# Attention tiles in pairs: one visit of the PE for two tiles, in a kernel of chunked attention and a low-rank mixer

## The chip, the cores and the metric

The kernel runs on one core of a Trainium2 chip. The metric is the device time of one launch, in microseconds (us). The profile shows TensorE as PE (matrix products) and PEld (loading of weights), VectorE as DVE, ScalarE as ACT, GpSimd as POOL, and SyncE as SP, which here only issues DMAs. A wait on a DMA queue's own issue is written SPq.

## The reference, cut to what matters

```python
B, H, S, D = 8, 8, 576, 64          # q, k, v; chunks of 64 rows
scores = scale * q_c @ k_c.T        # 64 x 64 for each chunk and head
attn = exp(scores - max) / (sum + 1e-9)
x = (attn @ v_c), heads side by side        # 8 x 576 x 512
h = x.transpose @ U @ V                     # rank 32, along the sequence
u = x + h.transpose
out = u + relu(u @ w_ch1) @ w_ch2           # 512 -> 2048 -> 512
```

All of it is float32 outside. The kernel splits the operands of the large products into a high and a low part and uses three products for one.

## The kernel before, in words

Two batches make a pair, and the kernel goes through four pairs (`pr` 0 to 3). The 1152 rows of a pair are nine tiles of 128 rows (`t` 0 to 8), and the tiles are three groups of three (`g` 0 to 2).

**The long work** is the last line of the reference, u through 2048 hidden columns. A group takes 16 blocks (`f`), and a block is 12 matmuls into one PSUM bank (`hidden`, tile `h`, L846), a relu on ACT that leaves the high part (`hh`, L854), a DVE instruction that leaves the low part (`hl`, L859), and 3 times 3 matmuls that add to three PSUM banks (`project_out`, tiles `o`, L872). The `o` of a block come after the `hidden` of the next one, so that the relu has time. Of each three `o` matmuls the third reads `hl`. After a group's last block DVE adds the three banks to x (L884) and SP sends x to the output (L887).

**The work beside it** belongs to the next pair. A tile's q and k are brought into blocks of 32 by DMAs on ACT's queue (`permute`), loaded by SP (`Tile.load`, tiles `qn` and `kn`, L695; tile 4 lies across two batches and takes four DMAs where the others take two) and transposed on DVE (`Tile.turn`, L703). Then PE makes the scores (32 matmuls of 64x64, L720), DVE subtracts the maximum (L733, L734), ACT takes the exponential (L740), DVE transposes it (`turn_ex`, L751) and sums it (`sums`, L745 to L747), SP writes it to DRAM in four DMAs (`put_ex`, L758) and reads it back in four (`get_ex`, L765, tile `eT`), and PE makes the values (32 more such matmuls, L773), which DVE scales into x (L785). `load_v` on POOL brings v (L710). The scores and values of a tile share two PSUM banks (`as`). When x is there, a projection per batch follows (`plan_proj`: `xh` on ACT, `xl` on DVE, two matmuls a tile into one bank, L586 and L587), then for each tile the mixer (`plan_mix`: one or two matmuls into a bank `u`, L633; an add on DVE, L639; a transpose on DVE, L808; four DMAs out, L816; one back, tile `uf`, L822; and a split into `uth` on ACT, L835, and `utl` on DVE, L836). `uth` and `utl` are the operands of `hidden`.

**What sets the order.** Every engine runs its instructions in the order in which the program lists them. Pair 0's attention and its first two groups are listed by a planner (`order`). There, two `hidden` in a row are often followed by two blocks of `o`. From group 2 of pair 0 on, plain loops list the work. In both, places are counted in steps: a block is four steps, one ahead of each of its three `o` groups and one behind them. Pair 0's groups 0 and 1 are steps 0 to 127 (`FIRST` = 128), group 2 is 128 to 191, and pair `pr` begins at `pr * PAIR` = 192 `pr`. The side work is put into a table by step (`at`), and the loops run what the table holds for a step.

**A visit** is what PE does for attention at one step. Before, `both` makes the values of one tile and the scores of the next in two banks; 28 visits serve the 27 tiles of pairs 1 to 3, the first with scores alone and the last with values alone. DVE's share of a visit is listed right there: two times maximum and subtraction, then two scalings.

**The pools.** PSUM has eight banks under one tag: three are held by the `o` sums, one or two by `h`, and `as`, `y` and `u` take the others for a while. `slot` buffers of 2 KB a partition (`NS` of them) hold all the small tiles, and `x` has `NX` buffers, freed when the output's DMA has read them.

Of the kernel before, what the change touches and what calls it, by code (L numbers as in the profile page):

```python
# [21 lines left out]
def kernel(  # L22
# [23 lines left out]
    NT = 2 * S // P  # L46
    GT = 3
    RUN = 8
    FAST = 3
    NX = 10  # L50
    NS = 8
    TB = 32
    k_in = k
    NQ = P // TB
# [5 lines left out]
    NPAIR = B // 2  # L60
# [10 lines left out]
    def bank(name):  # L71
        return psum.tile([P, 512], F32, tag="bank", name=name)
# [919 lines left out]
    def at(s, *runs):  # L992
        agenda.setdefault(s, []).extend(runs)

    def plan_tile(pr, t, s, before):
        a = Tile(pr, t)
        at(before + 2 if before >= s - 15 else s - 9, a.load)
        at(s - 4, a.turn)
        at(s + 1, a.load_v)
        at(s + 2, a.turn_ex, a.sums)  # L1000
        at(s + 3, a.put_ex)
        at(s + 6, a.get_ex)
        return a

    def plan_mix(pr, t, s, get=None):
        m = Mix(pr, t)
        at(s, m.low_rank, m.add)
        at(s + 1, m.turn)
        at(s + 2, m.put)
        at(s + 5 if get is None else get, m.get)  # L1010
        at(s + 10 if get is None else get + 8, m.split)

    def plan_proj(pr, e, i, s):
        if i == 0:
            projs[pr, e] = project_ops(pr, e, [None] * NT)[0]
        h, lo, product, *rest = projs[pr, e][i]
        at(s, h.run)
        at(s + 1, lo.run)
        at(s + (5 if i == 4 else 3), product.run, *(z.run for z in rest))

    projs = {}

    chain = [((1, t), FIRST + s) for t, s in enumerate((-51, -33, -11, 2, 15, 28, 42))]
    for pr in range(1, NPAIR):
        base = pr * PAIR
        chain += [((pr, 7), base + 4), ((pr, 8), base + 18)]
        if pr < NPAIR - 1:
            chain += [((pr + 1, t), base + s) for t, s in enumerate((34, 54, 74, 94, 114, 138, 157))]
    chain.append((None, (NPAIR - 1) * PAIR + 32))

    made = {}
    prev = None
    before = 0
    for key, s in chain:
        now = plan_tile(*key, s, before) if key else None

        def both(prev=prev, now=now):
            ps = [bank("as") for e in range(2)]
            if prev:
                prev.values(ps)  # L1040
            if now:
                now.scores(ps)
                now.softmax()
            if prev:
                prev.scaled()

        at(s, both)
        if prev:
            made[prev.pr, prev.t] = s
        prev, before = now, s  # L1050

    for pr in range(1, NPAIR):
        base = pr * PAIR
        if pr > 1:
            for z, e in enumerate(range(2)):
                for k in range(8):
                    at(base - PAIR - 26 + 42 * z + 5 * k, lambda pr=pr, e=e, k=k: permute(pr, e, [k]))
        s = made[pr, 4] + 1
        for i in range(5):
            plan_proj(pr, 0, i, s if i == 4 else s - 9 + 2 * i)  # L1060
        for t in range(3):
            plan_mix(pr, t, s + 8 + 2 * t)
        s = made[pr, 8] + 1
        for i in range(5):
            plan_proj(pr, 1, i, s if i == 4 else s - 9 + 2 * i)
        for t in range(3, 6):
            plan_mix(pr, t, s + 8 + 2 * (t - 3))
        for t in range(6, 9):
            plan_mix(pr, t, base + NF * 4 + 6 + 8 * (t - 6))

    for t in range(6, 9):
        plan_mix(0, t, FIRST - 45 + 2 * (t - 6), FIRST - 25 + t - 6)

    now = 0
    for o in plan:
# [55 lines left out]
```

## Time and profile before

| | |
|---|---|
| three timed runs | 935.1, 935.91, 936.25 us; median 935.91 |
| the profiled execution | 936.13 us, of which the span from the first to the last instruction is 934.4 |
| granted PE clock, mean | 0.996 |
| busy: DVE, ACT, POOL | 49%, 24%, 9% of the span |
| `h` matmuls, L846, 2304 | 338 ns each from start to end, started about every 175 ns |
| `o` matmuls, L872, 1728 | 396 ns each, started about every 233 ns |
| attention matmuls of pairs 1 to 3, L720 and L773 | 864 each; every matmul of the program appears as two |

Times are from the profiled execution; the matmuls overlap, so their starts say what one costs. In a row of the timeline stand the start, the length, the engine, the line and operation, the tile written and the tiles read, the shape and the count; brackets give idle time ahead of it and what ended that.

### The profile page before, as it was taken

How to read it: one execution, taken by the hardware profiler on the slowest of the kernel's cores; microseconds unless marked ns; L12 is line 12 of the kernel's file. 1: busy time of each engine (PE TensorE's matmuls, PEld its weight loads, DVE VectorE, ACT ScalarE, POOL GpSimd, SP SyncE). 2: the span in 40 equal slices, each digit the busy share in tenths (PEclk: the TensorE clock that was granted, in tenths of full speed). 3: DMA queues.
4: the chain of work that ended last, by engine and by line, in shares of the span. 5: the costliest groups of instructions: out<-in, count | busy, mean ns of one | idle time of the engine just before them, and what ended most of it. 6: DMA issues, size and time to landing. Idle time of an engine off the chain costs nothing.

```text
span 934.4 us, 16689 instructions
## 1 busy us (share of the span) xinstructions
PE 915.3 (98%) x6764; PEld 809.5 (87%) x6764; DVE 458.3 (49%) x901; ACT 227.1 (24%) x399; POOL 86.0 (9%) x153
## 2 busy tenths in 40 slices
PE   7799999999999999999999999999999999999998
PEld 6569888888898888888889888888889889999987
DVE  4699897464635565534524455534542533321111
ACT  5566671112221221112111222111221121111110
POOL 7000001121121111111110111020120100000000
PEclk9899999999999999999999999999999999999999
DMA  9972784764385574432555565432350312200000
GB/s 199 221 267 90 192 219 92 163 159 92 82 187 129 105 166 116 107 61 80 125 100 125 110 126 151 114 79 60 87 126 1 92 23 68 79 23 1 34 0 34
DMA packets 274396, 100.11 MB, mean 107 GB/s; under 512 B 198864, under 2 KB 260848, under 8 KB 274320
## 3 DMA queue, kind: packets, MB, share of 16 engines
q1 hardware_dynamic: 158528, 75.79, 31.7%
q10 hardware_dynamic: 111360, 14.16, 9.7%
q0 software_dynamic: 4432, 9.10, 3.8%
q8 instruction: 53, 0.87, 0.4%
q14 instruction: 23, 0.19, 0.1%
HBM read 74.63 MB, written 38.54 MB: 121 GB/s over the span
## 4 chain that ended last, share of the span: by engine, by line
PE 88%; DVE 5%; DMA 3%; ACT 2%; issue 1%; POOL 1%; SPq 0%; ACTq 0%; DVEq 0%; POOLq 0%
PE o L872 41%; PE h L846 40%; PE as L773 2%; PE as L720 1%; DMA qkv<-in_q_dram 1%; DVE w L376 1%; PE u L633 1%; DMA qkv<-in_v_dram 1%; DVE wraw L102 1%; PE y L592 1%; PE y L587 1%; DVE wroom L105 1%; DMA wraw<-in_moe_w_ch_dram 1%; PE y L586 1%; POOL qkv L419 1%
## 5 line engine op out<-in xcount | busy, mean ns | idle before, releaser
L846 PE MATMUL h<-uth,w 128*128 128x384 f32 x1536 | 424.1, 338 | 0.0
L872 PE MATMUL o<-w,hh 128*128 128x512 f32 x1152 | 363.8, 397 | 0.4 <-ACT hh L854 0.4
L859 DVE SCALAR_TENSOR_TENSOR hl<-h,hh 128x384 fp32r<-128x384 f32 x192 | 106.6, 556 | 382.3 <-ACT hh L854 382.2
L846 PEld LDWEIGHTS h<-uth,w 128*128 128x128 f32 x1536 | 281.1, 188 | 8.1 <-issue 0.2
L846 PE MATMUL h<-utl,w 128*128 128x384 f32 x768 | 259.5, 338 | 0.0
L872 PEld LDWEIGHTS o<-w,hh 128*128 128x128 f32 x1152 | 212.3, 188 | 35.8 <-ACT hh L854 1.1
L872 PE MATMUL o<-w,hl 128*128 128x512 f32 x576 | 227.8, 395 | 1.7 <-DVE hl L859 1.7
L854 ACT ACTIVATE hh<-h 128x384 fp32r<-128x384 f32 x192 | 94.2, 491 | 537.4 <-PE h L846 537.3
L846 PEld LDWEIGHTS h<-utl,w 128*128 128x128 f32 x768 | 144.2, 188 | 8.2 <-issue 0.2
L872 PEld LDWEIGHTS o<-w,hl 128*128 128x128 f32 x576 | 108.3, 188 | 29.6 <-DVE hl L859 4.1
L710 POOL DMA_DIRECT2D vn<-in_v_dram x108 | 66.0, 619 | 644.6 <-PE y L587 132.2
L740 ACT ACTIVATE ex<-ex 128x512 f32<-128x512 f32 x27 | 17.1, 633 | 97.6 <-DVE ex L734 88.1
L733 DVE TENSOR_REDUCE mx<-as 128x4 f32<-128x256 f32 x54 | 22.6, 419 | 29.2 <-PE as L720 29.2
L884 DVE TENSOR_TENSOR x<-o,x 128x512 f32<-128x512 f32 x48 | 30.5, 678 | 5.1 <-PE o L872 5.0
L639 DVE TENSOR_TENSOR x<-u,x 128x512 f32<-128x512 f32 x36 | 24.1, 671 | 8.6 <-PE u L633 8.6
L836 DVE TENSOR_TENSOR utl<-uf,uth 128x512 fp32r<-128x512 f32 x30 | 20.5, 683 | 8.9 <-ACT uth L835 8.9
L734 DVE TENSOR_TENSOR ex<-as,mx 128x256 f32<-128x256 f32 x54 | 22.9, 424 | 1.9
L773 PEld LDWEIGHTS as<-vn,eT 64*64 64x64 f32 x864 | 15.1, 134 | 9.1 <-issue 9.1
L808 DVE STREAM_TRANSPOSE xb<-x 128x512 f32<-128x512 f32 x30 | 21.2, 706 | 0.6
L376 DVE TENSOR_TENSOR w<-wroom,w 128x1024 fp32r<-128x1024 f32 (+1 forms) x19 | 19.7, 1051 | 3.0 <-ACT w L373 2.9
L579 DVE TENSOR_TENSOR xl<-x,xh 128x512 fp32r<-128x512 f32 x30 | 20.1, 681 | 1.0 <-ACT xh L575 0.7
L92 ACT ACTIVATE wroom<-wraw 128x1024 f32<-128x1024 f32 (+1 forms) x19 | 18.9, 996 | 6.7 <-DMA wraw<-in_moe_w_ch_dram 4.0
(93 smaller groups left out, 527.8 us busy)
## 6 DMA issues: line engine op xcount, KB each, us to landing
wraw<-in_moe_w_ch_dram SPq DMA_DIRECT2D x32, 512.0 KB, 5.8
out_dram<-x SPq DMA_DIRECT2D x36, 256.0 KB, 2.2
xs<-xb SPq DMA_DIRECT2D x120, 64.0 KB, 1.8
uf<-xs SPq DMA_DIRECT2D x30, 256.0 KB, 2.8
qblocks<-in_q_dram ACTq DMA_DIRECT2D x24, 288.0 KB, 4.4
kblocks<-in_k_dram ACTq DMA_DIRECT2D x24, 288.0 KB, 4.2
vn<-in_v_dram POOLq DMA_DIRECT2D x108, 64.0 KB, 2.8
exs<-exb SPq DMA_DIRECT2D x108, 64.0 KB, 1.8
```

Of the source, the lines that this page charges most:

```text
L376: nc.vector.tensor_sub(st["w"][:, 1, cols], v, st["w"][:, 0, cols])
L639: nc.vector.tensor_add(x, st["u"], x)
L710: nc.gpsimd.dma_start(self.vn[e * C : (e + 1) * C, c], v[b + 2 * self.pr, HP * e : HP * (e + 1), s0 : s0 + C, :].rearrange("h s d -> s h d"),)
L733: nc.vector.reduce_max(mx[:, e], self.sc[e].rearrange("p (h k) -> p h k", k=C), axis=AX.X)
L734: nc.vector.tensor_sub(self.ex[:, e].rearrange("p b h k -> p h b k"), self.sc[e].rearrange("p (h b k) -> p h b k", b=2, k=TB), mx[:, e].un ...
L773: nc.tensor.matmul(ps[e][cs, (HP + hp) * C : (HP + hp + 1) * C], lhsT=self.eT[rows, hp, 2 * c : 2 * c + 2, :].rearrange("p a i -> p (a i)" ...
L808: nc.vector.transpose(self.xb.rearrange("p g (c t) -> p c g t", t=TB), x_of[self.pr, self.t].rearrange("p (c g k) -> p c g k", g=NQ, k=TB),)
L846: nc.tensor.matmul(ps[:, :GN], lhsT=w[:, z, cc], rhs=u[:, cc, :], start=(n == 0), stop=(n == 3 * NCC - 1))
L854: nc.scalar.activation(hh, ps[:, :GN], AF.Relu)
L859: nc.vector.scalar_tensor_tensor(hl, ps[:, :GN], 0.0, hh, op0=ALU.max, op1=ALU.subtract)
L872: nc.tensor.matmul(acc[j], lhsT=h[:, js], rhs=w2[f][:, z], start=(first and i == 0), stop=(final and i == 2),)
L884: nc.vector.tensor_add(x, ps, x)
```

## The change

A visit now takes the scores of two tiles and the values of the two tiles before them, in four PSUM banks, and the five groups of a pair (2, 2, 2, 2 and 1 tiles) are visited at five steps (`CALLS` for pair 1, `TIMES` for the others). There are 16 visits, and scores come ahead of values. The steps of loads, transposes, sums, puts and gets follow from the step of the visit; where the next visit is less than 30 steps away, `turn_ex` and `sums` come from 2 and 4 steps behind the visit on, else from 13 and 15. The projections start behind the fourth and the next pair's first visit, and the mixers behind them. `permute` starts 10 steps earlier. Pair 0's last three mixers begin 5 steps earlier, and their reading back and splitting come 12 steps later (steps 115 to 117 and 123 to 125). `NX` goes from 10 to 9 and `NS` from 8 to 9. The planner's own order for pair 0 is the same up to the first visit.

```diff
@@ -47,8 +47,8 @@
     GT = 3
     RUN = 8
     FAST = 3
-    NX = 10
-    NS = 8
+    NX = 9
+    NS = 9
     TB = 32
     k_in = k
     NQ = P // TB
@@ -992,16 +992,6 @@
     def at(s, *runs):
         agenda.setdefault(s, []).extend(runs)
 
-    def plan_tile(pr, t, s, before):
-        a = Tile(pr, t)
-        at(before + 2 if before >= s - 15 else s - 9, a.load)
-        at(s - 4, a.turn)
-        at(s + 1, a.load_v)
-        at(s + 2, a.turn_ex, a.sums)
-        at(s + 3, a.put_ex)
-        at(s + 6, a.get_ex)
-        return a
-
     def plan_mix(pr, t, s, get=None):
         m = Mix(pr, t)
         at(s, m.low_rank, m.add)
@@ -1016,60 +1006,68 @@
         h, lo, product, *rest = projs[pr, e][i]
         at(s, h.run)
         at(s + 1, lo.run)
-        at(s + (5 if i == 4 else 3), product.run, *(z.run for z in rest))
+        at(s + 4, product.run, *(z.run for z in rest))
 
     projs = {}
 
-    chain = [((1, t), FIRST + s) for t, s in enumerate((-51, -33, -11, 2, 15, 28, 42))]
+    CALLS = (FIRST - 34, FIRST - 14, FIRST + 10, FIRST + 30, PAIR + 6)
+    TIMES = (26, 70, 134, 154, 198)
+    chain = []
     for pr in range(1, NPAIR):
-        base = pr * PAIR
-        chain += [((pr, 7), base + 4), ((pr, 8), base + 18)]
-        if pr < NPAIR - 1:
-            chain += [((pr + 1, t), base + s) for t, s in enumerate((34, 54, 74, 94, 114, 138, 157))]
-    chain.append((None, (NPAIR - 1) * PAIR + 32))
+        for i, s in enumerate(CALLS if pr == 1 else [(pr - 1) * PAIR + z for z in TIMES]):
+            chain.append((s, [Tile(pr, t) for t in range(2 * i, min(2 * i + 2, NT))]))
+    chain.append(((NPAIR - 1) * PAIR + TIMES[0], []))
 
     made = {}
-    prev = None
-    before = 0
-    for key, s in chain:
-        now = plan_tile(*key, s, before) if key else None
-
-        def both(prev=prev, now=now):
-            ps = [bank("as") for e in range(2)]
-            if prev:
-                prev.values(ps)
-            if now:
-                now.scores(ps)
-                now.softmax()
-            if prev:
-                prev.scaled()
-
-        at(s, both)
-        if prev:
-            made[prev.pr, prev.t] = s
-        prev, before = now, s
+
+    def visit(prev, now):
+        ps = [[bank("as") for e in range(2)] for _ in range(max(len(prev), len(now)))]
+        for a, z in zip(now, ps):
+            a.scores(z)
+        for a, z in zip(prev, ps):
+            a.values(z)
+        for z in range(len(ps)):
+            if z < len(now):
+                now[z].softmax()
+            if z < len(prev):
+                prev[z].scaled()
+
+    prev = []
+    for i, (s, now) in enumerate(chain):
+        for z, a in enumerate(now):
+            at(s - 19 + 6 * z, a.load)
+            at(s - 13 + 6 * z, a.turn)
+        at(s, lambda prev=prev, now=now: visit(prev, now))
+        for a in prev:
+            made[a.pr, a.t] = s
+        if now:
+            after = chain[i + 1][0]
+            s1 = s + 2 if after - s < 30 else s + 13
+            for z, a in enumerate(now):
+                at(s1 + z, a.turn_ex)
+                at(s1 + 2 + z, a.sums)
+                at(s1 + 2 + z, a.put_ex)
+                at(max(s1 + 5, after - 14) + z, a.load_v)
+                at(max(s1 + 7, after - 12) + z, a.get_ex)
+        prev = now
 
     for pr in range(1, NPAIR):
         base = pr * PAIR
         if pr > 1:
             for z, e in enumerate(range(2)):
                 for k in range(8):
-                    at(base - PAIR - 26 + 42 * z + 5 * k, lambda pr=pr, e=e, k=k: permute(pr, e, [k]))
-        s = made[pr, 4] + 1
-        for i in range(5):
-            plan_proj(pr, 0, i, s if i == 4 else s - 9 + 2 * i)
-        for t in range(3):
-            plan_mix(pr, t, s + 8 + 2 * t)
-        s = made[pr, 8] + 1
-        for i in range(5):
-            plan_proj(pr, 1, i, s if i == 4 else s - 9 + 2 * i)
-        for t in range(3, 6):
-            plan_mix(pr, t, s + 8 + 2 * (t - 3))
+                    at(base - PAIR - 36 + 50 * z + 5 * k, lambda pr=pr, e=e, k=k: permute(pr, e, [k]))
+        for e in range(2):
+            s = made[pr, 4 + 4 * e] + 2
+            for i, z in enumerate((0, 2, 3, 5, 6)):
+                plan_proj(pr, e, i, s + z)
+            for t in range(3):
+                plan_mix(pr, 3 * e + t, s + 14 + 2 * t)
         for t in range(6, 9):
             plan_mix(pr, t, base + NF * 4 + 6 + 8 * (t - 6))
 
     for t in range(6, 9):
-        plan_mix(0, t, FIRST - 45 + 2 * (t - 6), FIRST - 25 + t - 6)
+        plan_mix(0, t, FIRST - 50 + 2 * (t - 6), FIRST - 13 + t - 6)
 
     now = 0
     for o in plan:
```

**Where rows move, first place.** DVE around the second visit (step 114, the values of tiles 0 and 1 and the scores of tiles 2 and 3 of pair 1, while pair 0 is in block 13 of its group 1). In the names, `hl_1_14` is `hl` of group 1, block 14, and `mx_2`, `ex_2`, `exb_2`, `sm_2` and `x_0` carry the tile's number. Before, one tile stands between `hl` of block 13 and that of block 14:

```order
L859 SCALAR_TENSOR_TENSOR hl_1_13_2205<-h_1_13_2169,hh_1_13_2192 128x384
L733 TENSOR_REDUCE mx_2_2252<-as 128x4
L734 TENSOR_TENSOR ex_2_2251<-as,mx_2_2252 128x4x2x32
L733 TENSOR_REDUCE mx_2_2252<-as 128x4
L734 TENSOR_TENSOR ex_2_2251<-as,mx_2_2252 128x4x2x32
L785 TENSOR_TENSOR x_1_2258<-as,sm_1_2054 128x256 x2
L751 STREAM_TRANSPOSE exb_2_2269<-ex_2_2251 128x512
L745 TENSOR_REDUCE sm_2_2271<-ex_2_2251 128x4 x2
L746 TENSOR_SCALAR sm_2_2271<-sm_2_2271 128x8
L747 RECIPROCAL sm_2_2271<-sm_2_2271 128x8
L859 SCALAR_TENSOR_TENSOR hl_1_14_2308<-h_1_14_2280,hh_1_14_2306 128x384
```

Now the tail of that stretch on DVE reads as follows (ahead of it stand five rows of tile 2's softmax and tile 0's scaling):

```order
L733 TENSOR_REDUCE mx_3_2265<-as 128x4
L734 TENSOR_TENSOR ex_3_2264<-as,mx_3_2265 128x4x2x32
L785 TENSOR_TENSOR x_1_2271<-as,sm_1_2029 128x256 x2
L751 STREAM_TRANSPOSE exb_2_2279<-ex_2_2254 128x512
L751 STREAM_TRANSPOSE exb_3_2286<-ex_3_2264 128x512
L745 TENSOR_REDUCE sm_2_2293<-ex_2_2254 128x4 x2
L746 TENSOR_SCALAR sm_2_2293<-sm_2_2293 128x8
L747 RECIPROCAL sm_2_2293<-sm_2_2293 128x8
L745 TENSOR_REDUCE sm_3_2303<-ex_3_2264 128x4 x2
L746 TENSOR_SCALAR sm_3_2303<-sm_3_2303 128x8
L747 RECIPROCAL sm_3_2303<-sm_3_2303 128x8
L859 SCALAR_TENSOR_TENSOR hl_1_14_2347<-h_1_14_2319,hh_1_14_2345 128x384
```

The work of two tiles, with both transposes and both sums, now stands ahead of `hl` of block 14. Further ahead, at the first visit, DVE now has the mixer's add for tile 7, the transposes of q and k of tile 0, and the mixer's transpose between `hl` of block 8 and `hl` of block 9 of group 0, where block 9's followed block 8's at once; the add and transpose of tile 6's mixer stand ahead of both.

**Second place.** DVE right behind that, up to the first block of pair 0's group 2 (`utl_2` is the low operand of that group, made in three thirds from `uf_6`, `uf_7` and `uf_8`). Before, the last third stands ahead of `hl` of block 13:

```order
L859 SCALAR_TENSOR_TENSOR hl_1_12_2184<-h_1_12_2154,hh_1_12_2182 128x384
L836 TENSOR_TENSOR utl_2_2149<-uf_7_2118,uth_2_2148 128x4x4x32
L703 STREAM_TRANSPOSE qT_2_2199<-qn_2_2136 128x512
L703 STREAM_TRANSPOSE kT_2_2200<-kn_2_2137 128x512
L836 TENSOR_TENSOR utl_2_2149<-uf_8_2126,uth_2_2148 128x4x4x32
L859 SCALAR_TENSOR_TENSOR hl_1_13_2205<-h_1_13_2169,hh_1_13_2192 128x384
```

Now it stands behind the transposes of tile 4's q and k:

```order
L859 SCALAR_TENSOR_TENSOR hl_1_14_2347<-h_1_14_2319,hh_1_14_2345 128x384
L859 SCALAR_TENSOR_TENSOR hl_1_15_2357<-h_1_15_2332,hh_1_15_2352 128x384
L836 TENSOR_TENSOR utl_2_2363<-uf_6_2274,uth_2_2362 128x4x4x32
L836 TENSOR_TENSOR utl_2_2363<-uf_7_2281,uth_2_2362 128x4x4x32
L703 STREAM_TRANSPOSE qT_4_2384<-qn_4_2313 128x512
L703 STREAM_TRANSPOSE kT_4_2385<-kn_4_2314 128x512
L836 TENSOR_TENSOR utl_2_2363<-uf_8_2288,uth_2_2362 128x4x4x32
L884 TENSOR_TENSOR x_3_565<-o_3_2169,x_3_565 128x512
```

And SP's queue, where `qn_4` and `kn_4` are what those transposes read. Before:

```order
L758 DMA exs_2_2313<-exb_2_2269 32x4x128 x4
L765 DMA eT_2_2328<-exs_2_2313 128x4x32 x4
L887 DMA out_dram<-x_3_565 128x512
L887 DMA out_dram<-x_4_712 128x512
L887 DMA out_dram<-x_5_782 128x512
L695 DMA qn_4_2442<-qblocks_1380 128x4x64
L695 DMA kn_4_2443<-kblocks_1381 128x4x64
L695 DMA qn_4_2442<-qblocks_1653 128x4x64
L695 DMA kn_4_2443<-kblocks_1654 128x4x64
```

Now:

```order
L822 DMA uf_6_2274<-xs_6_1805 128x512
L822 DMA uf_7_2281<-xs_7_1836 128x512
L822 DMA uf_8_2288<-xs_8_1849 128x512
L758 DMA exs_2_2298<-exb_2_2279 32x4x128 x4
L758 DMA exs_3_2308<-exb_3_2286 32x4x128 x4
L695 DMA qn_4_2313<-qblocks_1380 128x4x64
L695 DMA kn_4_2314<-kblocks_1381 128x4x64
L695 DMA qn_4_2313<-qblocks_1653 128x4x64
L695 DMA kn_4_2314<-kblocks_1654 128x4x64
```

The loads of tile 4 are now behind the eight puts of tiles 2 and 3, and `utl`'s last third is behind the loads.

**Third place.** PE in block 0 of pair 1's group 1 (step 70 of the pair; pair 2 has the same rows). Before, the mixer's matmul `u_6` stands alone between `o` matmuls:

```order
L872 MATMUL o_4_4007<-w_642,hh_1_0_3963 128x512 x2
L872 MATMUL o_4_4007<-w_642,hl_1_0_3965 128x512
L633 MATMUL u_6_4015<-ys_1_3686,vst 128x512
L872 MATMUL o_5_4018<-w_642,hh_1_0_3963 128x512 x2
L872 MATMUL o_5_4018<-w_642,hl_1_0_3965 128x512
L846 MATMUL h_1_2_4024<-uth_1_3818,w_1087 128x384
L846 MATMUL h_1_2_4024<-utl_1_3819,w_1087 128x384
```

Now a visit stands right ahead of it:

```order
L872 MATMUL o_4_4002<-w_642,hh_1_0_3962 128x512 x2
L872 MATMUL o_4_4002<-w_642,hl_1_0_3964 128x512
L720 MATMUL as<-kT_2_3896,qT_2_3895 64x64 x16
L720 MATMUL as<-kT_3_3946,qT_3_3945 64x64 x16
L773 MATMUL as<-vn_0_3880,eT_0_3906 64x64 x16
L773 MATMUL as<-vn_1_3890,eT_1_3914 64x64 x16
L633 MATMUL u_6_4094<-ys_1_3679,vst 128x512
L872 MATMUL o_5_4097<-w_642,hh_1_0_3962 128x512 x2
L872 MATMUL o_5_4097<-w_642,hl_1_0_3964 128x512
L846 MATMUL h_1_2_4103<-uth_1_3848,w_1087 128x384
```

The visit's four banks and `u_6`'s bank are taken at one step, ahead of the next `hidden`.

## The prediction

> **What bounds the kernel now.** I read the busy shares of the page first, then the chain of the work that ended last, then the table of waits.
>
> ```profile
> PE 915.3 (98%) x6764; PEld 809.5 (87%) x6764; DVE 458.3 (49%) x901; ACT 227.1 (24%) x399; POOL 86.0 (9%) x153
> 264.08 2.09 PE o L872 x9
> 266.18 2.11 PE h L846 x12
> PE o L872 <- DVE hl L859: 1.7, 4, 0.7
> PE y L587 <- DVE xl L579: 0.2, 1, 0.2
> ```
>
> PE is busy 98% of 934.4 us, and the chain (rows two and three) is an unbroken alternation of 9 `o` in 2.09 and 12 `h` in 2.11: a block is 4.20 us, a step 1.05, an `o` matmul 0.233. In the waits (sum, count, longest) PE waits for `hl` only four times, 1.7 us in all. So time is won only by PE spending less, and lost wherever PE is made to wait. The granted clock comes last, below.
>
> **Term 1: fewer visits.** What a visit costs PE is read from the timeline, first one with a single batch of 32 small matmuls, then one with two.
>
> ```profile
> 148.60 0.39 PE L872 MATMUL o<-w,hl 128*128 128x512 f32 x1
> 150.34 0.34 PE L846 MATMUL h<-uth,w 128*128 128x384 f32 x1
> ...
> 343.62 0.40 PE L872 MATMUL o<-w,hl 128*128 128x512 f32 x1
> 343.95 0.69 PE L773 MATMUL as<-vn,eT 64*64 64x64 f32 x32
> 344.47 0.65 PE L720 MATMUL as<-kT,qT 64*64 64x64 f32 x32
> 345.04 0.73 PE L872 MATMUL o<-w,hh 128*128 128x512 f32 x2
> 345.84 0.34 PE L846 MATMUL h<-uth,w 128*128 128x384 f32 x1
> ```
>
> From the last `o` ahead of the visit to the next `h` is 1.74 us with one batch (148.60 to 150.34) and 2.22 with two (343.62 to 345.84). Four `o` starts of 0.233 lie in each, so the visit costs 0.81 and 1.29. A batch is thus 0.48, and 0.33 is fixed per visit. The batches stay 54; visits go from 28 to 16: 12 x 0.33 = **-4.0 us**. Bounds: 0, if the fixed part goes with batches, to -4.4 (a switch to small matmuls and back read from the starts alone: 0.52 and 0.57 against 0.48, 0.13, is smaller, so I take the difference of whole visits). A visit of four batches lasts 0.52 + 0.48 + 0.48 + 0.57 = 2.05 from its first matmul to the next `o`. I call its first matmul V.
>
> **Term 2: the first visit, pair 0.** DVE now has the mixer's add, two transposes and the mixer's transpose between two `hl`.
>
> ```profile
> L639 DVE TENSOR_TENSOR x<-u,x 128x512 f32<-128x512 f32 x36 | 24.1, 671 | 8.6 <-PE u L633 8.6
> L703 DVE STREAM_TRANSPOSE qT<-qn 128x512 f32<-128x512 f32 x27 | 18.8, 698 | 2.2 <-DMA qn<-qblocks 2.2
> L703 DVE STREAM_TRANSPOSE kT<-kn 128x512 f32<-128x512 f32 x27 | 18.5, 684 | 2.0 <-DMA kn<-kblocks 1.5 <-DMA xs<-xb 0.4
> L808 DVE STREAM_TRANSPOSE xb<-x 128x512 f32<-128x512 f32 x30 | 21.2, 706 | 0.6
> L859 DVE SCALAR_TENSOR_TENSOR hl<-h,hh 128x384 fp32r<-128x384 f32 x192 | 106.6, 556 | 382.3 <-ACT hh L854 382.2
> L633 PE MATMUL u<-ys,vst 128*128 128x512 f32 x40 | 14.9, 400 | 0.0
> ...
> 154.55 0.62 PE L872 MATMUL o<-w,hh 128*128 128x512 f32 x2
> 155.47 0.50 PE L872 MATMUL o<-w,hl 128*128 128x512 f32 x1 [0.30 <-DVE hl L859]
> ```
>
> The add follows tile 7's `u` matmul (0.40). Then 0.671 + 0.698 + 0.684 + 0.706 + 0.556 = 3.3 us, less four overlaps of about 0.08 between neighbours: `hl` of block 9 is ready 0.40 + 3.0 = 3.4 after `u` starts. PE comes to the `o` that reads it after `u` (0.23), six `o` (1.40), another `u` (0.23) and two more `o` (0.47): 2.33. So PE waits 1.1. Before, it waited at the same block: from the pair's start 154.55 to 155.47 is 0.92 where two starts take 0.47, so 0.45 goes. Net **+0.6** (bounds 0 and 1.1).
>
> **Term 3: the second visit, `hl` of block 14.** DVE is to do two tiles' whole share, transposes and sums too, ahead of one `hl`.
>
> ```profile
> 345.15 0.42 DVE L733 TENSOR_REDUCE mx<-as 128x4 f32<-128x256 f32 x1 [0.56 <-PE as L720]
> 346.74 0.74 DVE L785 TENSOR_TENSOR x<-as,sm 128x256 f32<-128x256 f32 x2
> ...
> 198.13 0.71 DVE L751 STREAM_TRANSPOSE exb<-ex 128x512 f32<-128x512 f32 x1
> 199.83 0.51 DVE L859 SCALAR_TENSOR_TENSOR hl<-h,hh 128x384 fp32r<-128x384 f32 x1
> ```
>
> The maximum starts 0.68 behind the start of its scores (344.47 to 345.15). Of the four batches DVE waits for tile 2's scores (first) and tile 0's values (third), so I count from a batch a little later: V + 1.68, 0.68 behind the third batch's start at V + 1.00. A tile takes 345.15 to 347.48, 2.33, less 0.08 of overlap: two tiles 4.5, so V + 6.2. Transpose and sums take 198.13 to 199.83, 1.70 a tile: 3.4, V + 9.6, and `hl` 0.56: V + 10.1. PE wants it after the visit (2.05), the `o` of block 13 (2.09), two `h` (4.22) and two `o` starts (0.47): V + 8.8. **+1.3** (0.3, if DVE starts with the first batch, to 1.5).
>
> **Term 4: `utl` of pair 0's group 2, the largest loss.** Its last third stands on DVE behind tile 4's transposes, these behind tile 4's loads, and these on SP behind the puts of tiles 2 and 3.
>
> ```profile
> 207.09 0.52 SPq L695 DMA_DIRECT2D qn<-qblocks  x1
> 209.13 0.63 SPq L695 DMA_DIRECT2D kn<-kblocks  x1
> ...
> 226.21 1.79 SPq L758 DMA_DIRECT2D exs<-exb  x4
> 228.10 2.07 SPq L765 DMA_DIRECT2D eT<-exs  x4
> ...
> qn<-qblocks SPq DMA_DIRECT2D x6, 128.0 KB, 3.3
> kn<-kblocks SPq DMA_DIRECT2D x6, 128.0 KB, 3.8
> ...
> L836 DVE TENSOR_TENSOR utl<-uf,uth 128x512 fp32r<-128x512 f32 x30 | 20.5, 683 | 8.9 <-ACT uth L835 8.9
> ```
>
> Tile 2's transpose ends at V + 6.2 + 0.71 = 6.9. Four puts hold SP 1.89 (226.21 to the next issue, 228.10); eight, 3.8: V + 10.7. The fourth load of a four-part tile issues 2.04 behind its first (207.09 to 209.13): V + 12.7. It lands 3.8 later, the median of the same half-tile load (rows of the DMA view: KB, us to landing): V + 16.5. Then `kT` 0.684 and `utl` 0.683, less 0.08: V + 17.8. PE, after term 3's wait, passes the `o` at V + 10.1, has seven more of block 14 and nine of block 15 (16 x 0.233 = 3.7) and one `h` (0.18): it wants `utl` at V + 14.0. **+3.7.** Before, the third stood ahead of `hl` of block 13 and nobody waited. With the landing at 3.3 (the row of `qn`) it is +3.2; with two landings' difference above, +4.3. Below that it falls only if puts issue faster than in this row.
>
> **Term 5: banks, step 70 of pairs 1 and 2.** A visit takes four of the eight banks, the sums three, `h` one; `u_6` right behind it takes the next bank that comes free, and the `h` after it a further one. The visit's first bank is free when the first scaling ends: from the maximum's start 345.15 to 346.74 plus about half of 0.74, 2.0, so V + 3.7. PE wants the next `h` at V + 2.05 + 0.34 for `u_6` + 0.70 for three `o` = 3.1. So 0.6 each, **+1.2** (bounds 0 and 2).
>
> **Term 6: the granted clock.** PE idles 3.7 us in one piece (term 4). The start of the trace shows what such a piece did:
>
> ```profile
> 28.06 0.66 PE L431 MATMUL ps_kT<-ident,qkv 128*128 128x128 f32 x4
> 31.68 1.09 PE L431 MATMUL ps_qT<-ident,qkv 128*128 128x128 f32 x4 [2.96 <-DMA qkv<-in_q_dram]
> ...
> 26.75:30.16 3.41, 1.80 (x66) 1.36 (x56) 2.28 (x10) 0.53 (x2) 0.00 (x0) 1.00 1.19 221
> 30.16:33.57 3.41, 1.89 (x6) 1.25 (x6) 1.83 (x2) 3.15 (x4) 0.00 (x0) 0.50 0.44 90
> 33.57:36.99 3.42, 3.42 (x36) 1.67 (x35) 1.45 (x5) 0.00 (x0) 0.00 (x0) 0.50 1.03 209
> ```
>
> After an idle of 2.96 us four transposes took 1.09 instead of 0.66, and the windows (length, PE busy, the other engines, then the granted clock, DMA share and GB/s) give 0.50 through 36.99. Busy PE at half clock does half its work, so a stretch of 3.41 at 0.50 costs 1.7. Term 4's idle is longer than that one, and PE's work behind it is dense, as in the second of the two stretches. I take one such stretch less a little of it spent idle: **+1.5** (bounds 0, and 2.7, if the clock stays down for the 5.3 us that it did from 31.68 to 36.99).
>
> The Trainium skill, "TensorE: Matmul & The Clock Gate", Part 1 on the clock gate, says that the clock falls to half only after a whole idle window of about 3.4 us and that these windows run free of the program. By its words an idle of 3.7 us seldom covers one, and the sum would be without this term; the 2.96 us above, which brought half the clock though shorter than a window, speaks against so strict a reading.
>
> **Term 7.** Before's one wait of `y` for `xl`, 0.2 us, loses its cause as products now come four steps behind: **-0.2**.
>
> **Costed at nothing.** In the steady loops `hl` behind a visit waits only for two tiles' softmax and scaling, V + 6.2 + 0.56 = 6.7; PE wants it after the visit, three `o` (0.70 at most), `h`, `o`, `h` and two `o` starts: V + 2.05 + 0.70 + 2.11 + 2.09 + 2.11 + 0.47 = 9.5, room 2.8. The transposes come from 2 or 13 steps on, one to a step, beside PE's 1.05. Over the shortest gap between visits, 20 steps or 21 us, eight puts and eight gets stand in line:
>
> ```profile
> xs<-xb SPq DMA_DIRECT2D x120, 64.0 KB, 1.8
> uf<-xs SPq DMA_DIRECT2D x30, 256.0 KB, 2.8
> eT<-exs SPq DMA_DIRECT2D x108, 64.0 KB, 2.4
> ```
>
> Transposes are done by V + 8.2, puts issued by V + 12.0 (2 x 1.89) and landed 1.8 later, as `xs`, at V + 13.8; the gets take 2 x 2.07, V + 17.9, and land 2.4 later, V + 20.3. The next visit's values come at V + 21 + 2.05 + 1.0: room about 3. If it is gone, a visit costs the tile's lateness. `NX` 9 and `NS` 9, and `permute` earlier: transfers beside others; nothing on PE waits for them before.
>
> **Sum.** -4.0 + 0.6 + 1.3 + 3.7 + 1.2 + 1.5 - 0.2 = +4.1 us, on the profiled execution's 936.13 (span 934.4): 940.2. That execution lies 0.2 above the median of the runs, so the median of the changed kernel is put at **940.0 us**.
>
> **Rivals.**
> - *The clock stays up*, as the page read strictly would have it: everything but term 6, 938.5 us. For it, the idle is one piece only; against it, the 2.96 us row.
> - *Tile 4's loads are early* (the other side, not slower). Place: SP between `put_ex` of tile 3 and DVE's `kT`. If loads land by V + 12.8, 3.7 earlier than worked out, PE does not stop at group 2, and terms 4 and 6 go together: 940.0 - 5.2 = 934.8. This takes puts and loads issued in about half of their time and a landing under 3; no row of SP shows that, but the chain of five durations is where I could be most wrong. If terms 2 and 3 shrink too it is faster than before.
> - *The fixed part goes with batches or operands, not visits*: then term 1 is 0 and the change does not save what it is made to save: 944.0. Against it: one and two batches differ by 0.48 and not by 0.81.
> - *A new wait at the start of pair 1*: the third tile's mixer is put at step 180, read back at 183 and split at 188 with `h` ahead of step 192. Put 1.89, landing 1.8, reading back 2.8 and the split's 0.683 are 7.2 of 12.6 us (12 steps); if eight puts and eight gets of the visits (3.8 + 4.1) slip in between, 2.5 us are missing, of which those that SP issues while the first put lands cost nothing, so I put up to 1.5 on it: 941.5.
>
> **How the numbers follow.** Forecast 0.58, clock stays 0.14, loads early 0.12, wait at pair 1 0.09, no saving 0.07. The second and fourth lie in the range; left out are most of the third and the last, under 0.2. The terms' bounds about the forecast are some -3 and +2.5, and so I take **935.7 to 942.7 us**. What a measurement of this kernel can tell from no change is about 0.2%, 1.9 us: same is 934.0 to 937.8. Slower: 0.53 of the forecast, 0.10 of the clock, the fourth and the last: 0.79. Same: 0.05, 0.04 and half of the third: 0.15. Faster: the other half, 0.06.
>
> **What would show it.** In the waits after: `h` L846 on `utl` L836 once with 3 to 4 us; `o` on `hl` twice with about 1; `h` on a bank twice with 0.6. A half-clock stretch behind the long wait. A visit of four batches at 2.05. A last `utl` of pair 0 that does not end behind `kT` of tile 4, or visits that cost as much per batch as before, would make the prediction wrong.

## The result and the profile after

| | before | changed |
|---|---|---|
| median of five runs | 936.13 us | 945.57 us |
| lowest to highest | 935.1 to 936.25 | 944.65 to 946.59 |
| span of the profiled execution | 934.4 us | 943.8 us |

The ratio is 1.0109, 95% interval 1.0096 to 1.0122: the change makes the kernel slower by 1%. The forecast was 940.0 us (935.7 to 942.7). The sign was right, and the loss is more than twice the one forecast.

PE's waits in the changed kernel come first, from the table of waits (sum in us, count, longest):

```profile
PE h L846 <- DVE utl L836: 5.0, 2, 4.7
PE o L872 <- DVE hl L859: 3.3, 4, 0.9
PE h L846 <- ACT uth L835: 3.3, 1, 3.3
PE h L846 <- DVE x L785: 1.1, 2, 0.6
```

The three rows on `h` are new, 9.4 us together, and the waits for `hl` went from 1.7 to 3.3. The timeline of PE shows where they stand, each with what follows:

```profile
155.74 0.50 PE L872 MATMUL o<-w,hl 128*128 128x512 f32 x1 [0.94 <-DVE hl L859]
200.51 0.50 PE L872 MATMUL o<-w,hl 128*128 128x512 f32 x1 [0.86 <-DVE hl L859]
209.38 0.69 PE L846 MATMUL h<-utl,w 128*128 128x384 f32 x1 [4.71 <-DVE utl L836]
214.89 0.62 PE L872 MATMUL o<-w,hh 128*128 128x512 f32 x2
286.92 0.45 PE L846 MATMUL h<-uth,w 128*128 128x384 f32 x1 [3.26 <-ACT uth L835]
287.64 0.69 PE L846 MATMUL h<-utl,w 128*128 128x384 f32 x1 [0.28 <-DVE utl L836]
291.17 0.62 PE L872 MATMUL o<-w,hh 128*128 128x512 f32 x2
374.93 0.42 PE L846 MATMUL h<-uth,w 128*128 128x384 f32 x1 [0.52 <-DVE x L785]
```

In this order: the first visit, the second visit, the start of pair 0's group 2, **the start of pair 1** (286.92), and the bank wait behind the visit at step 70. The two long waits are followed by PE at half clock, as the windows show (length, PE busy, four other engines, granted clock, DMA share, GB/s):

```profile
204.00:208.00 4.00, 0.67 (x4) 0.25 (x2) 0.55 (x1) 0.00 (x0) 0.00 (x0) 1.00 1.15 237
208.00:212.00 4.00, 2.62 (x8) 2.62 (x9) 3.12 (x6) 0.00 (x0) 0.00 (x0) 0.63 0.36 103
284.00:288.00 4.00, 0.80 (x2) 0.55 (x3) 1.85 (x3) 1.11 (x2) 0.00 (x0) 0.94 1.21 200
288.00:292.00 4.00, 4.00 (x15) 3.87 (x15) 0.11 (x1) 0.49 (x1) 0.00 (x0) 0.63 1.06 144
```

From 209.38 to the next `o` at 214.89, 23 `h` matmuls take 5.51 us; at 0.176 each they would take 4.05. So 1.46 us went to the clock. From 286.92 to 291.17, 12 `h` take 4.25, of which 2.11 is their usual time and 0.28 a wait: 1.86 us to the clock.

### The profile page after: what moved, and what is told of

Same layout as the page of the kernel before. It is cut to its first block, busy times and chain, and to the rows that moved or that the text cites. A ratio compares the mean times of both kernels' runs of the same rounds, so it can differ in the third digit from the quotient of the medians.

```text
span 943.8 us, 16657 instructions
## 1 busy us (share of the span) xinstructions
PE 914.4 (97%) x6764; PEld 812.9 (86%) x6764; DVE 456.1 (48%) x901; ACT 225.5 (24%) x399; POOL 86.0 (9%) x153
## 4 chain that ended last, share of the span: by engine, by line
PE 88%; DMA 5%; DVE 3%; POOL 1%; issue 1%; SPq 1%; ACT 1%; ACTq 0%; POOLq 0%; DVEq 0%
PE h L846 41%; PE o L872 40%; PE as L720 2%; PE as L773 1%; DMA wraw<-in_moe_w_ch_dram 1%; DMA qkv<-in_q_dram 1%; DMA qkv<-in_v_dram 1%; PE u L633 1%; PE y L587 1%; PE y L586 1%; DMA kblocks<-in_k_dram 1%; POOL qkv L419 1%; DMA kn<-kblocks 0%; DVE wraw L102 0%; DMA xs<-xb 0%
## 5 line engine op out<-in xcount | busy, mean ns | idle before, releaser
L846 PEld LDWEIGHTS h<-utl,w 128*128 128x128 f32 x768 | 145.3, 189 | 13.8 <-DVE utl L836 5.6
L835 ACT CAST uth<-uf 128x512 fp32r<-128x512 f32 x30 | 18.2, 616 | 28.7 <-DMA uf<-xs 28.7
L703 DVE STREAM_TRANSPOSE qT<-qn 128x512 f32<-128x512 f32 x27 | 18.9, 700 | 9.2 <-DMA kn<-kblocks 5.3
L102 DVE SCALAR_TENSOR_TENSOR wraw<-wraw 128x1024 uint32<-128x1024 uint32 (+1 forms) x19 | 20.0, 1050 | 0.7 <-ACT wraw L95 0.7
```

The costliest lines, as they stand in the source:

```text
L102: lambda: nc.vector.scalar_tensor_tensor(lo, hi, 0x80000000, lo, op0=ALU.bitwise_and, op1=ALU.bitwise_or),
L846: nc.tensor.matmul(ps[:, :GN], lhsT=w[:, z, cc], rhs=u[:, cc, :], start=(n == 0), stop=(n == 3 * NCC - 1))
```

## What holds the two long waits

**Pair 0's group 2 (term 4).** The visit, SP's and DVE's rows in the timeline of the changed kernel:

```profile
190.47 1.16 PE L720 MATMUL as<-kT,qT 64*64 64x64 f32 x64
...
197.35 3.73 SPq L758 DMA_DIRECT2D exs<-exb  x8
201.31 0.52 SPq L695 DMA_DIRECT2D qn<-qblocks  x1
203.22 0.64 SPq L695 DMA_DIRECT2D kn<-kblocks  x1
...
207.45 0.71 DVE L703 STREAM_TRANSPOSE qT<-qn 128x512 f32<-128x512 f32 x1 [5.33 <-DMA kn<-kblocks]
208.68 0.65 DVE L836 TENSOR_TENSOR utl<-uf,uth 128x512 fp32r<-128x512 f32 x1
```

The visit is at V = 190.47. The puts start at V + 6.9, the fourth load issues at V + 12.75, and DVE stands idle 5.33 us until it lands, at V + 17.0. This is the chain of the prediction, step by step, but for two sizes: the last load takes 4.2 us to land where 3.8 was put, and both transposes start only then, not `kT` alone. So `utl` comes at V + 18.9 and not 17.8.

**Pair 1's start (the fourth rival).** SP's timeline ahead of the wait at 286.92, then two rows of ACT, the second of which ends it:

```profile
263.38 4.21 SPq L758 DMA_DIRECT2D exs<-exb  x8
269.25 3.70 SPq L816 DMA_DIRECT2D xs<-xb  x8
273.07 0.52 SPq L695 DMA_DIRECT2D qn<-qblocks  x1
273.69 0.57 SPq L695 DMA_DIRECT2D kn<-kblocks  x1
274.36 0.57 SPq L822 DMA_DIRECT2D uf<-xs  x1
275.02 4.45 SPq L816 DMA_DIRECT2D xs<-xb  x4
279.51 3.89 SPq L822 DMA_DIRECT2D uf<-xs  x2
...
273.19 0.55 ACTq L678 DMA_DIRECT2D kblocks<-in_k_dram  x1
286.25 0.62 ACT L835 CAST uth<-uf 128x512 fp32r<-128x512 f32 x1 [1.74 <-DMA uf<-xs]
```

The first mixers of pair 1 now follow the puts of tiles 6 and 7. The third mixer's four puts, which the prediction priced at 1.89, take 4.45 to issue. The last of the four is what is late, as SP's timeline from 278 us on and the table of SP's waits show:

```profile
279.16 0.30 SPq L816 DMA_DIRECT2D xs<-xb  x1
SPq L816 <- DMA kblocks<-in_k_dram: 2.8, 1, 2.8
```

The first three issue by 276.38, at the usual pace. The fourth waits 2.8 us for the landing of a DMA that has nothing to do with it: a part of `permute` for pair 2, `kblocks`, which ACT issued at 273.19 (the row above) and which landed at 279.14. In the trace the put waits for the semaphore (the counter that tells of a landing) that this DMA raises, and raises the same one itself. So the last reading back issues at 283.06, and `uth` starts at 286.25, where PE wanted it at about 283.7 (286.92 less 3.26). The window in which the puts issue, with the DMA share and GB/s last:

```profile
275.00:280.00 5.00, 5.00 (x28) 4.55 (x27) 0.56 (x1) 0.49 (x1) 1.75 (x3) 1.00 1.16 287
```

The DMAs move more here, 287 GB/s, than in the stretches of 5 us beside it (224 and 97). Two explanations were tried in runs: the mixers' place (late by steps, behind the sums on DVE and the puts on SP) and the traffic (tile 8's loads, 512 KB, between the mixers' puts). The wait for `kblocks` is a third, read from the traces alone.

## The experiments

Times are medians; ratios are to the kernel before on the same chip, with their intervals. The kernel before took 936.13 us beside the changed kernel and 934.86 to 935.15 beside the experiments. So a difference to the changed kernel (1.0109) is taken from the two ratios; the medians alone would give about 1 us more of gain. The starts of the program wait for inputs, and there profiled executions differ: the first `o` matmul came at 61.06 us in the changed kernel, at 62.50 before and at 63.68 in the run with earlier mixers. A difference of 1 or 2 us between two profiles is read from places behind it.

**Tile 4's transposes behind `utl`.** (The edit moves tile 4's, not tile 5's.)

```diff
-            at(s - 13 + 6 * z, a.turn)
+            at(s - (9 if (a.pr, a.t) == (1, 4) else 13) + 6 * z, a.turn)
```

> The changed kernel with one thing moved: the transposes of pair 1's tiles 4 and 5 come 4 steps later, behind the last third of utl of pair 0's group 2. Theory A (the wait of 4.71 us of h for utl comes from utl's place on DVE behind those transposes, and the half clock behind it, 1.5 us, comes from that wait): both go, 945.6 - 6.2 = about 939.4 us. Rival (the read-back uf_8 itself is late, since SP and the DMAs are full there): utl is late at its new place as well, a wait of 2 us or more stays, 943 us or more. Rival (the clock falls for another reason): 940.9 us.

Measured: 939.66 us, 1.0051 [1.0036, 1.0066]. The wait of `h` for `utl` is gone from the table, and the window over that place has clock 1.00. Theory A holds: by the ratios 5.4 us for the wait of 4.71 and the half clock. The wait at pair 1's start stayed (3.24).

**The mixers of pair 1 earlier.**

```diff
-                plan_mix(pr, 3 * e + t, s + 14 + 2 * t)
+                plan_mix(pr, 3 * e + t, s + (10 if (pr, e) == (1, 0) else 14) + 2 * t)
```

> The changed kernel with the first three mixers of pair 1 put 4 steps earlier (ahead of tile 6's and 7's transposes, sums and puts instead of behind them); nothing else is moved by hand. Theory A (the wait of 3.26 us of h for uth at pair 1's start comes from the late place of these mixers, on DVE behind the sums and on SP behind eight puts; the half clock behind it costs 1.7 us more): 945.6 - 5.2 = about 940.3 us. Rival (the DMAs are full at this place, and the read-back lands late wherever it is put): the wait shrinks by less than half, 943 us or more.

Measured: 945.56 us, 1.0104 [1.0078, 1.013]: no gain in the time. The expectation missed; the trace says why in part:

```profile
265.91 0.50 PE L633 MATMUL u<-ys,vst 128*128 128x512 f32 x1 [1.39 <-DVE ys L615]
289.10 0.44 PE L846 MATMUL h<-uth,w 128*128 128x384 f32 x1 [0.51 <-ACT uth L835]
```

The wait for `uth` fell from 3.26 to 0.51, and behind it PE runs at full clock. But `u` now comes before its operand and waits 1.39 for `ys`. Against the changed kernel this run stands 3.4 us later at the first `o` of pair 0's group 2 (218.30 against 214.89) and 0.8 later at the last `o`: 2.6 us are gained behind that place, and they were lost ahead of it, at the start above all (63.68 against 61.06).

**Both.** 

> Both moves of the two other kernels in one. Theory A: the two stretches are apart, so the gains add up: 945.6 - 11.4 = 934.2 us, a little faster than the kernel before. Rival (one wait hides the other, so that what is behind slips to the same end): 938 us or more.

Measured: 937.27 us, 1.0024 [1.0015, 1.0034]. That is 2.4 us less than with the transposes alone, so the earlier mixers do gain, less the new wait for `ys`. 3 us short of the expectation.

**Both, and the last mixers away from the visit at step 70.**

```diff
-            plan_mix(pr, t, base + NF * 4 + 6 + 8 * (t - 6))
+            plan_mix(pr, t, base + NF * 4 + 9 + 8 * (t - 6))
```

> As the kernel with both moves, and the last three mixers of pairs 1 to 3 begin 3 steps later, so that the first of them no longer takes its bank right behind a visit of four. Theory A (h waits for a bank there in pairs 1 and 2, 0.69 us each, and u 0.1): 1.6 us less than with both moves, about 932.6 us. Rival (that wait only moves, or the later read-back is late for group 2): no gain or a loss against the kernel with both moves.

Measured: 935.36 us, 0.9999 [0.9988, 1.001]: 1.9 us less than without it, and the row of `h` waiting for `x` (a scaling that frees the bank) is gone. Theory A holds.

**Sums and puts of the second visit later.** This leaves tile 4's transposes ahead of `utl` on DVE and takes the eight puts from ahead of tile 4's loads on SP. It also lets `hl` of block 14 come ahead of tile 3's transpose and both tiles' sums on DVE.

```diff
-            s1 = s + 2 if after - s < 30 else s + 13
+            s1 = s + {FIRST - 14: 5}.get(s, 2 if after - s < 30 else 13)
```

> The changed kernel with one number moved: at the second visit (step 114) the transposes and sums of tiles 2 and 3 begin 5 steps behind the visit and not 2, so their eight puts come behind tile 4's four loads on SP; tile 4's transposes stay ahead of the last third of utl on DVE. Theory A (the loads were late for standing behind the puts): the loads land before DVE comes to them, h waits no more for utl, the half clock behind it goes too, and hl of block 14 (0.9 us) is no longer late: 945.6 - 7.0 = about 938.6 us. Rival (the loads of a four-part tile land late wherever they stand): only the 0.9 us go, 944.5 us or so.

Measured: 938.81 us, 1.0043 [1.003, 1.0056]: by the ratios 6.2 us less than the changed kernel, 7.0 expected. SP and PE in this run:

```profile
192.99 0.52 SPq L695 DMA_DIRECT2D qn<-qblocks  x1
195.02 1.05 SPq L695 DMA_DIRECT2D kn<-kblocks  x1
197.62 3.74 SPq L758 DMA_DIRECT2D exs<-exb  x8
...
204.71 0.44 PE L846 MATMUL h<-utl,w 128*128 128x384 f32 x1 [0.98 <-DVE utl L836]
```

The loads now issue ahead of the eight puts, DVE no longer waits for them, and of the 4.71 us 0.98 stay, which are DVE's own queue. So what made `utl` late was the loads' place behind the puts.

**Puts of the fourth visit later.** The same edit with `{FIRST + 30: 22}`.

> The changed kernel with one number moved: at the fourth visit (step 158) the transposes, sums and puts of tiles 6 and 7 begin 22 steps behind the visit and not 13, behind the first mixers of pair 1, which keep their steps. Theory A (uth of pair 1 is late because these mixers stand on DVE and SP behind the sums and the eight puts): the mixers' puts issue some 4 us earlier, the wait of 3.26 us and the half clock behind it go: about 941 us. Rival (the mixers' steps are too late by themselves, and the DMAs are full there): 2 us or more of the wait stay, 944 us or more.

Measured: 951.06 us, 1.017 [1.0155, 1.0185]: 5.7 us slower than the changed kernel by the ratios, where 4.6 less was expected. SP and PE:

```profile
269.78 5.56 SPq L816 DMA_DIRECT2D xs<-xb  x8
275.57 0.52 SPq L695 DMA_DIRECT2D qn<-qblocks  x1
276.19 0.58 SPq L695 DMA_DIRECT2D kn<-kblocks  x1
277.52 1.86 SPq L816 DMA_DIRECT2D xs<-xb  x4
282.10 0.34 SPq L822 DMA_DIRECT2D uf<-xs  x1
282.54 4.07 SPq L758 DMA_DIRECT2D exs<-exb  x8
286.72 0.48 SPq L822 DMA_DIRECT2D uf<-xs  x1
...
292.19 0.69 PE L846 MATMUL h<-uth,w 128*128 128x384 f32 x1 [5.93 <-ACT uth L835]
```

The step I chose put the eight puts between the second and the third reading back, so the third issues 4.6 us behind the second, at 286.72. The mixers did start earlier: their first puts issue 16.5 us before PE comes to pair 1 (269.78 and 286.25), against 14.4 in the changed kernel (269.25 and 283.65). The gain is lost in that queue, and in a wait of 2.6 us of the second reading back for `kblocks`. So the experiment does not tell the two theories apart as meant; it shows that with the eight puts ahead of the last reading back PE waits 2.7 us longer. It also speaks against the loads as the cause by themselves: tile 8's two loads stand right ahead of the third mixer's puts here too, and these take 1.86.

**The two later sums and the later last mixers.** 

> The two moves of the sums and puts (5 steps behind the second visit, 22 behind the fourth), and the last three mixers of pairs 1 to 3 from 9 steps into group 1 on. Theory A: the gains add up, 945.6 - 7.0 - 4.6 - 1.6 = about 932.4 us, faster than the kernel before. Rival (fewer visits save nothing, and a kernel without the new waits only comes back to the kernel before): 935 to 936 us.

Measured: 941.6 us, 1.0068 [1.0055, 1.0081], 9 us above the expectation. It carries the fourth visit's late puts, and the wait for `uth` is 6.04 here too.

**The same, and tile 0's transposes behind `hl` of block 9.**

```diff
-            at(s - 13 + 6 * z, a.turn)
+            at(s - (11 if (a.pr, a.t) == (1, 0) else 13) + 6 * z, a.turn)
```

> As the kernel with three moves, and the transposes of pair 1's tile 0 come 2 steps later, behind hl of block 9 of pair 0's group 0. Theory A (the wait of 0.94 us there is these two transposes' and no other's): 0.9 us less than with three moves, about 931.5 us. Rival (the add of tile 7's mixer and its transpose alone make hl late): 0.2 us less or nothing.

Measured: 940.9 us, 1.0058 [1.0045, 1.0072]: 0.7 us less than without it, within what the runs scatter, but the wait of 0.95 us at this block is gone from the timeline. Theory A for the place; the size is not settled by the times.

**Only tile 8's load and transposes later.**

```diff
-            at(s - 19 + 6 * z, a.load)
-            at(s - 13 + 6 * z, a.turn)
+            at(s - (14 if (a.pr, a.t) == (1, 8) else 19) + 6 * z, a.load)
+            at(s - (8 if (a.pr, a.t) == (1, 8) else 13) + 6 * z, a.turn)
```

> The changed kernel with the load and transposes of pair 1's tile 8 five steps later: 512 KB that SP issued between the mixers' puts and their reading back go behind all three readings. Theory B (what makes uth of pair 1 late is traffic: the third mixer's four puts took 4.45 us to issue, behind these loads): the wait of 3.26 us shrinks by 2 us or more and the half clock behind it goes with it, 942 us or less. Theory A (the mixers' steps alone are too late): the wait stays, 945 us.

Measured: 942.12 us, 1.0082 [1.0069, 1.0095]: 2.5 us less than the changed kernel by the ratios; in the profiles the stretch from the first `o` to the last is 4.8 us shorter (873.6 against 878.4). SP and PE:

```profile
276.32 1.89 SPq L816 DMA_DIRECT2D xs<-xb  x4
278.38 3.86 SPq L822 DMA_DIRECT2D uf<-xs  x2
...
285.97 0.44 PE L846 MATMUL h<-utl,w 128*128 128x384 f32 x1 [0.28 <-DVE utl L836]
```

The loads issue from 282.39 on. The mixers kept their steps, the third's four puts took 1.89 in place of 4.45, and the wait for `uth` is gone with its half clock. Theory A in its strict form falls: with the same steps the wait is gone when the loads are not in between. That the loads hurt by their bytes, theory B's reason, is not shown. What is gone from SP is the fourth put's wait of 2.8 us for `kblocks`; in the run with the puts of the fourth visit later, where the loads are in place, that put has no such wait either. Moving the loads changes both the traffic and which earlier DMA a put has to wait for, and no run tells these apart.

**Seven moves in one.** The expectation counts tile 5's transposes, which the edit again leaves in place; it makes six moves. New in it are the products of pair 1's first projection, closer together, so that `ys` is there for the early mixers:

```diff
-            for i, z in enumerate((0, 2, 3, 5, 6)):
+            for i, z in enumerate((0, 1, 2, 3, 4) if (pr, e) == (1, 0) else (0, 2, 3, 5, 6)):
```

> Every move so far that paid, in one: transposes of pair 1's tile 0 two and of tiles 4 and 5 four steps later, sums and puts of the second visit five steps behind it, the first three mixers of pair 1 four steps earlier, the last three mixers of pairs 1 to 3 three steps later; and, new, the five products of pair 1's first projection at steps 4 to 8 behind its place and not 4 to 10, so that the early mixers do not wait for ys. Theory A: against the kernel with two moves and the later last mixers (0.9999 of before), the waits of o for hl (0.94 and 0.95 us), of u for ys (1.39) and of h for uth (1.0) go: about 4.3 us less than the kernel before, 931 us. Rival (fewer visits save nothing): 935 us.

Measured: 931.13 us, 0.9961 [0.9949, 0.9973]: 4.0 us faster than the kernel before in the medians, and by the ratios 13.8 faster than the changed one. The waits for `ys`, for `hl` at both visits and for the bank are gone; a wait of 1.08 for `uth` is left, which was to go.

**And tile 8's load later.** 

> The kernel with all moves that paid, and tile 8's load five steps later as well. Theory A: no wait is left there that this could shorten, so the same as without it, about 931 us. Theory B: 0.5 us less, if a wait for uth was left.

Measured: 931.67 us, 0.997 [0.9958, 0.9982], not told apart from the seven moves. The wait for `uth` is gone, but `o` waits 0.7 for `hh` in its stead.

**Scores and values in turns.**

```diff
-        for a, z in zip(now, ps):
-            a.scores(z)
-        for a, z in zip(prev, ps):
-            a.values(z)
+        for i, z in enumerate(ps):
+            if i < len(now):
+                now[i].scores(z)
+            if i < len(prev):
+                prev[i].values(z)
```

> The kernel with seven moves (0.9961 of the kernel before), with one more: in a visit the scores and the values take turns, tile by tile, where before both tiles' scores came ahead of both tiles' values. Theory A (a change from one batch to the next costs PE some 0.04 us between scores and values but 0.09 at the start of the second batch of scores): 0.05 to 0.1 us a visit, about 1 us in all, 930.1 us. Rival (what a visit costs lies in its entry and its exit alone): the same as without it, 931.1 us. Second rival (the DVE gets both tiles' scores later, and the bank of the first tile is free earlier): within 0.5 us either way.

Measured: 932.26 us, 0.9974 [0.9965, 0.9983]: no gain over the seven moves. The first rival holds: the nine visits with four batches cost 20.4 us together in this profile, and 20.3 without the edit.

## Why the prediction was right and wrong

- **What bounds it, and the sign:** right. Fewer visits save little, and new waits of PE cost more.
- **Term 1, mis-sized.** -4.0 forecast. A four-batch visit does last 2.05, from 442.13 to 444.18 in the timeline below, as five of the nine do; the others last 2.10 to 2.20. I summed over all visits of the loops what they add to the gaps around them (first gap, visit and the longer gap behind, less two usual ones): 34.3 us for the 27 before, 0.81 more for the first one, which the planner listed, and 32.2 us for the 16 after. So 2.9 were saved. The nine visits with four batches cost 2.28 each and not 2.25, and the five with three batches 1.92 where 0.33 + 3 x 0.48 gives 1.77.

```profile
442.13 1.16 PE L720 MATMUL as<-kT,qT 64*64 64x64 f32 x64
443.12 1.14 PE L773 MATMUL as<-vn,eT 64*64 64x64 f32 x64
444.18 0.74 PE L872 MATMUL o<-w,hh 128*128 128x512 f32 x2
```

- **Term 2, +0.6:** right. A wait of 0.94 (155.74) for one of 0.30.
- **Term 3, +1.3:** the mechanism is right, the size 0.86 (200.51). DVE was ready at V + 10.0, as worked out (V + 10.1); PE came there at V + 9.2 and not V + 8.8.
- **Term 4, +3.7:** the mechanism is right, shown by two experiments, one on DVE and one on SP; the size is 4.71, since the last load landed at V + 17.0 and not 16.5, and both transposes waited for it.
- **Term 5, +1.2:** right: 1.1 us in two waits, and 1.9 us when the mixer is moved away.
- **Term 6, +1.5:** 1.46 behind term 4's wait. So the rival in which the clock stays up falls. By the clock rule that the prediction cited (the Trainium skill, "TensorE: Matmul & The Clock Gate", Part 1) the clock falls after a whole idle window of about 3.4 us. So it would have stayed behind the wait of 3.26 us, which is shorter; here it fell behind that one and behind 4.71.
- **The step that failed: the fourth rival, a new wait at the start of pair 1, held to be no more than a chance of 0.09 and 1.5 us.** It cost 3.26 + 0.28 in waits and 1.86 in clock, 5.4 us. The place was named, but not what stood there. The rival had the eight puts and eight gets of the visits slip in between the third mixer's put and its reading back; in the trace the puts issue before the mixers' (263.38 to 267.59) and the gets behind them (from 283.51). What it had wrong is its sum, 7.2 us from the put to the split, begun at step 180. By the loops' 1.05 us a step, that step is at about 271.0, and SP comes to the put 4.0 later, at 275.02: the mixers' adds stand on DVE behind the sums of tiles 6 and 7, which was not counted, and on SP the put stands behind the puts of the first two, tile 8's loads and a reading back. From there the chain takes 11.9 us. The four puts take 4.45 and not 1.89, 2.8 of it the fourth put's wait for `kblocks`, of `permute`, which the prediction had costed at nothing; the reading back issues 3.6 later and not 1.8, and takes 3.2 and not 2.8. With the 4.0 that is 15.9 of the 12.6 us that the twelve steps give, 3.3 short: the wait measured. And no half clock was charged, though term 6 had the rule for it.
- **Term 7:** right, the wait is gone.

The measured terms: -2.9 + 0.6 + 0.9 + 4.7 + 1.1 + 1.5 + 5.4 - 0.2 = 11.1 us. The first `o` came 1.4 earlier in this execution, which leaves 9.7; the spans differ by 9.4. From the first `o` to the last, the two profiles differ by 11.0. Without the wait at pair 1 the measured terms come to +5.7, within the range: terms 1, 3 and 4 were each off by 0.4 to 1.1 us, and this one step put the time outside it.

Fewer visits do pay once the waits are away: the run called seven moves keeps all 16 visits and is 0.4% faster than the kernel before. In its profile the stretch from the first `o` to the last is 2.5 us shorter than before, and its visits cost 3.1 us less (32.0 against 35.1), so the gain is that of the visits. Whether the wait for `kblocks` goes when `permute` is put elsewhere was not tried: tile loads that come earlier need its blocks. The change moved the first batch's part of it by 10 steps, and its DMAs come every 5, so the kernel before has one at most of the same steps too. Which of the moves is needed beside the others was not tried one by one.

## What to carry to other kernels

When work is batched to save a fixed cost, the saving is small and sure, and the price lies where a batch of instructions and DMAs now stands ahead of something that the bounding engine will want: walk every queue to the next such operand. A queue of DMAs is not priced by its own issues alone: look in the table of waits for DMAs that wait for the landing of another queue's. Charge a wait of the bounding engine that is of some 2.3 us or more with a half clock behind it; how far that rule goes is said below.

## What the runs showed of the hardware

The clock falls behind shorter waits than I had thought. In the run with the later sums of the second visit, PE stood 2.35 us at pair 1's start and, after one `h`, 0.29 more:

```profile
279.83 0.44 PE L846 MATMUL h<-uth,w 128*128 128x384 f32 x1 [2.35 <-ACT uth L835]
281.89 0.83 PE L846 MATMUL h<-uth,w 128*128 128x384 f32 x2
```

A window of the same run, with the granted clock third from the end:

```profile
280.00:284.00 4.00, 3.71 (x14) 3.28 (x15) 0.58 (x2) 0.49 (x1) 0.00 (x0) 0.74 1.28 198
```

Full clock lasted 2 us longer, and then `h` pairs took 0.83 in place of 0.51. Waits of 1.08 and 0.28 at the same place, in the run with seven moves, left the clock at 1.00. In all runs, every one of the ten waits of 2.35 to 6.07 us behind the first `o` brought the half clock, and none of those up to 1.39 did. The length of the wait is not all that decides: at the start of the changed kernel, ahead of the first `o`, a wait of 2.40 us left the clock at 1.00:

```profile
32.80 0.63 PE L431 MATMUL ps_qT<-ident,qkv 128*128 128x128 f32 x4 [2.40 <-DMA qkv<-in_q_dram]
34.00:38.00 4.00, 3.31 (x73) 2.13 (x73) 3.87 (x7) 1.93 (x5) 0.00 (x0) 1.00 0.85 177
```

Nor does the price of a fall follow from the wait. The clock stood at 0.50 for 3.4 us at each of the two long waits of the changed kernel, for 6.8 us at a wait of 4.91 in the run with earlier mixers, and for 10.2 us at one of 5.93 in the run with the puts of the fourth visit later.
